# Inverting the first pair of chunks in 16x16 blocks joined by matmuls, with other PSUM banks and another early order, in a chunked delta-rule attention kernel

## The chip, the cores and the metric

One core of one Trainium2 chip. The metric is the device time of one launch in microseconds (us), given as the median of several runs; one further execution is profiled. TensorE (PE) multiplies matrices, VectorE (DVE) and ScalarE (ACT) work elementwise and move results out of PSUM, GpSimd (POOL) works elementwise beside DVE, SyncE (SP) issues transfers. PE's clock has two levels, 1.2 and 2.4 GHz; the profile shows the granted share of the higher one. All arithmetic is float32 or a split of a float32 number into two parts for the matmul.

## The reference

Three layers, one behind the other (sizes are batch 4, heads 8, 768 positions, head size 48; 3072 tokens of width 384):

```python
for t in range(S):                       # attention, per (batch, head)
    kt, vt, bt = k_n[:, :, t], v[:, :, t], beta[:, :, t, None]
    y[:, :, t] = einsum(q[:, :, t], state)
    state = state + bt * outer(kt, vt - state.T @ kt)
...
P = exp(x @ w_gate); 8 rounds of row and column normalisation
for e in range(8):                       # experts, 384 -> 1024 -> 384
    out += P[:, e:e+1] * (relu(x @ w1[e]) @ w2[e])
...
h = x @ w_in                             # 384 -> 2048
out = (h * cos(h)) @ w_out
```

## The kernel before, in words

The 768 positions are cut into 12 chunks of 64, called **units**; a unit holds its chunk of all 32 (batch, head) pairs. Inside a unit the recurrence is a lower triangular system of 64x64 per pair, done as two blocks of 32. Their inverses are made for two units at a time (units 0 and 1, 2 and 3, and so on): a tile holds one 32x32 system per partition and group, and `inv_ops` (L332 to L350) transposes the matrices into it (Nsys, L332), makes a unit triangle (L335, L339) and eliminates in 30 steps of a product (L346) and an addition (L350), 60 elementwise instructions. For the first pair all 60 run on DVE; for the later pairs they run on POOL, queued by the token `i`. `inv_dm` (L357) and `inv_tx` (L360) then transpose the inverse back into the tiles dm and tx.

The stages of a unit, with the letters that name them in the order string: T (L251, keys transposed, copied by ACT at L259), B (L277, Gram matrix of the keys; DVE and ACT combine the blocks at L302/L303, `gk_b` at L309 scales by beta, `gk_o` at L314 keeps the off-diagonal block Go), Q and q (queries transposed, and their Gram matrix, leaving DVE as Pp, L326), Z (`pe_Z1`, L368, dm times Go, copied out by ACT at L373), z (`pe_Z2`, L380, combined into Bs at L386 by ACT and L387 by DVE), K (`pe_KS`, L398, state times keys; DVE makes D from it at L414), k (L398, state times queries, "QS"), U (L426, out by DVE at L432), S (L441, state update at L446), P (L456, out by ACT at L461), X (L473, output transposed and split into two parts at L478/L479). `norm_sums` (L222 on ACT, L223 on DVE) and `norm_chain` (L231 to L238) make the keys' norms, `norm_scale` (L242) applies them; N is that chain for later units. G and g are the gate (L487, L491, and the small product L498).

K and q use the PSUM bank pair pab, Z1 and Z2 its two halves unless told otherwise: the D of a unit is read by DVE out of the bank that Z1 of the same unit writes next.

Everything up to unit 0's Z1 and Z2 is a hand-written prologue: loads on SP, ACT's and POOL's queues, sums and norms of units 0 and 1, their Gram products, the first inversion on DVE with parts of units 2 and 3 in between, POOL's inversion for units 2 and 3 (L335 on POOL), warm-up products on zeros (`warm`). Then `tick(u, seq)` walks a string of tokens for units 0 and 1 together, then for unit 2, then one string for odd and one for even units. Each engine takes its instructions in that order. The token m is one **half**: nine matmuls of 512 columns of expert 0, either the first layer h (L130, relu at L157/L158) or the second y (L151), on 512 tokens already through X, and a half is skipped when its tokens are not there yet (`done`). a, b and W split expert weights (L120 on ACT, L121 on DVE). Ahead of every token up to three queued POOL steps are emitted. Behind unit 11 the other experts follow, and then the last layer; that part takes most of the span and is the same in both kernels.

```python
elif c == "K":
    pe_KS(u)
elif c in "ZY":
    pe_Z1(u, *([p01[:, 0]] if early else []))
elif c == "r" and u + 1 < NU:
    inv_some(99)
    inv_dm(Xsys)
elif c == "i" and nxt["B"] < NU + 1 and u + 2 < NU:
    inv_q.extend(inv_ops(Nst, Nsys, Xsys, tmp, nc.gpsimd))
```

Of the kernel before, what the change touches and what calls it, by code (L numbers as in the profile page):

```python
# [34 lines left out]
def kernel(  # L35
# [555 lines left out]
    with tc.manual_schedule():  # L591
# [73 lines left out]
        gram(p23, KT[1], KT[1], True)  # L665
        n = [gk_n(0, pcd, n0), gk_n(1, p23, n0)]
        for u in range(2):
            gk_b(u, n[u], nc.vector)
        ops = inv_ops(n0, ns0, xs0, W0.rearrange("p s t -> p (s t)"), nc.vector)
        ops[0]()  # L670
        ops[1]()
        gk_o(0, pcd)
        gk_o(1, p23)
        for u in range(2, 4):
            norm_sums(u)
        for x in ops[2:8]:
            x()
        norm_chain(2, 4)
        for u in range(2, 4):
            norm_scale(u, nc.vector)  # L680
        nc.vector.transpose(out=beta_x, in_=bw[1].rearrange("p (u t) -> p u t", t=CB))
# [13 lines left out]
        pe_TQ(0, pab)  # L695
        load_q(1)
        pe_GQ(0, p01)
        for x in ops[14:]:
            x()
        inv_dm(xs0)  # L700
        inv_tx(xs0)
        warm(60)
        pe_KS(0)
        pe_Z1(0)
# [439 lines left out]
```

## Time and profile before

| | |
|---|---|
| median of 3 runs | 2311.76 us (2309.25 to 2312.98) |
| the profiled execution | 2312.32 us |
| its span | 2310.6 us, 37567 instructions |
| mean granted clock of PE | 0.972 |
| busy: PE, DVE, ACT, POOL | 2206.5 (95%), 996.1 (43%), 628.4 (27%), 476.3 (21%) |
| PE's busy tenths, first four of 40 slices (57.8 us each) | 5, 5, 7, 9 |

Times in the rows are us from the span's start. A line of a timeline reads: start, duration, engine, line of the kernel, operation, output<-inputs, shape, count of instructions in the row, and in brackets how long the engine stood idle before it and what released it. SPq is SP's queue of issued transfers. A line of the windows reads: stretch, its length, then the busy time (and count) of PE, PEld (weight loads), DVE, ACT and POOL, PE's granted clock as a share of 2.4 GHz, the busy share of the transfer engines, and GB/s. A line of the waits reads: who waited for whom, us in total, times, the longest.

### The profile page before, as it was taken

The numbers are of one execution on the slowest core, as the hardware profiler recorded it, in microseconds if no ns is written. First come the engines' busy times: TensorE is split into PE (matmuls) and PEld (weight loads), VectorE is DVE, ScalarE is ACT, GpSimd is POOL, SyncE is SP. The second block draws the span as 40 slices with busy tenths as digits, with TensorE's granted clock in tenths as the row PEclk, the third lists the DMA queues.
The fourth block names the chain that finished last, engine by engine and source line by source line (L and its number), as shares of the span: only waits on it lengthen the run. The fifth ranks groups of instructions, "written<-read, shape, count | busy, mean of one in ns | idle before, by whom it ended". The sixth has DMA issues, their size and how long they took to land.

```text
span 2310.6 us, 37567 instructions
## 1 busy us (share of the span) xinstructions
PE 2206.5 (95%) x16211; PEld 1843.4 (80%) x16211; DVE 996.1 (43%) x1613; ACT 628.4 (27%) x1017; POOL 476.3 (21%) x649
## 2 busy tenths in 40 slices
PE   5579999989999999999999999999999999999998
PEld 4467777768888888888888888888888878888887
DVE  7554452243235334334433433433232226666665
ACT  2233332231112112111111211211121126666565
POOL 5436445002122111111101110111011122221221
PEclk7789999999999999999999999999999999999999
DMA  4332322053212112101210211121021130000000
GB/s 80 84 77 64 78 71 55 32 191 118 73 42 81 34 37 78 41 29 50 78 32 28 85 40 37 49 61 37 17 69 41 60 110 1 14 14 14 15 14 14
DMA packets 167639, 123.87 MB, mean 54 GB/s; under 512 B 80208, under 2 KB 159568, under 8 KB 166704
## 3 DMA queue, kind: packets, MB, share of 16 engines
q1 hardware_dynamic: 161936, 97.36, 15.5%
q0 software_dynamic: 4448, 23.90, 3.0%
q8 instruction: 127, 2.08, 0.4%
q10 hardware_dynamic: 1088, 0.20, 0.1%
q14 instruction: 40, 0.33, 0.0%
HBM read 90.65 MB, written 30.77 MB: 53 GB/s over the span
## 4 chain that ended last, share of the span: by engine, by line
PE 90%; DVE 5%; issue 2%; ACT 2%; DMA 1%; POOL 0%; SPq 0%; POOLq 0%; ACTq 0%; DVEq 0%
PE ps L130 42%; PE ps L151 34%; PE ps L140 8%; PE ps L251 1%; PE ps L277 1%; PE ps L368 1%; PE ps L380 1%; PE ps L398 1%; DMA scr<-in_moe_w_dram 1%; DVE scr L350 1%; DVE W L346 1%; PE ps L426 0%; PE ps L652 0%; DMA ysc<-y 0%; DVE Nsys L332 0%
## 5 line engine op out<-in xcount | busy, mean ns | idle before, releaser
L130 PE MATMUL ps<-x,w1t 128*128 128x512 f32 x3564 | 877.5, 391 | 2.5 <-DVE h L158 1.4
L151 PE MATMUL ps<-h,w2t 128*128 128x512 f32 x3456 | 864.5, 395 | 0.0
L130 PEld LDWEIGHTS ps<-x,w1t 128*128 128x128 f32 x3564 | 669.0, 188 | 139.8 <-DVE h L158 2.1
L151 PEld LDWEIGHTS ps<-h,w2t 128*128 128x128 f32 x3456 | 654.7, 190 | 137.1
L158 DVE SCALAR_TENSOR_TENSOR h<-ps,h 128x512 fp32r<-128x512 f32 x384 | 265.5, 691 | 944.2 <-ACT h L157 944.1
L157 ACT ACTIVATE h<-ps 128x512 fp32r<-128x512 f32 x384 | 229.5, 598 | 1263.7 <-PE ps L130 1263.7
L939 POOL TENSOR_TENSOR acc<-acc,scr 128x512 f32<-128x512 f32 x126 | 165.9, 1317 | 1099.9 <-DVE scr L938 1099.9
L140 PE MATMUL ps<-w2t,h 128*128 128x384 f32 x720 | 138.5, 339 | 3.5 <-DVE acc L1019 1.5
L140 PEld LDWEIGHTS ps<-w2t,h 128*128 128x128 f32 x720 | 127.4, 188 | 13.2 <-ACT acc L1017 3.1
L995 DVE TENSOR_TENSOR tp<-tp,ps 128x512 f32<-128x512 f32 x96 | 66.1, 688 | 146.0 <-ACT tp L994 146.0
L130 PE MATMUL ps<-xb,w1t 128*128 128x512 f32 x432 | 113.7, 406 | 5.3 <-DVE xb L479 2.1
L981 POOL TENSOR_SCALAR tp<-tp 128x512 f32<-128x512 f32 x96 | 59.4, 619 | 256.8 <-ACT tp L980 256.6
L130 PEld LDWEIGHTS ps<-xb,w1t 128*128 128x128 f32 x432 | 79.5, 191 | 25.5 <-DVE xb L479 3.7
L938 DVE TENSOR_TENSOR scr<-ps,scr 128x512 f32<-128x512 f32 x126 | 86.0, 682 | 10.7 <-DMA scr<-pts 7.8
L140 PE MATMUL ps<-x,h 128*128 128x384 f32 x432 | 83.4, 339 | 0.0
L130 PE MATMUL ps<-x 128*128 128x512 f32 x324 | 81.8, 397 | 1.3 <-DVE scr L938 1.3
L1000 ACT ACTIVATE h<-tp 128x512 fp32r<-128x512 f32 x96 | 60.7, 632 | 76.9 <-DVE tp L995 70.2
L350 POOL TENSOR_TENSOR w1t<-w1t 128x30 f32<-128x30 f32 (+9 forms) x150 | 78.9, 526 | 11.8
L140 PEld LDWEIGHTS ps<-x,h 128*128 128x128 f32 x432 | 76.2, 188 | 5.6 <-DVE h L1005 2.4
L989 ACT ACTIVATE tp<-tp 128x512 f32<-128x512 f32 x96 | 60.7, 632 | 73.1 <-DVE tp L986 73.1
L346 POOL TENSOR_TENSOR w1t<-Nsys,w1t 128x30 f32<-128x30 f32 (+9 forms) x150 | 74.9, 500 | 11.3
L130 PEld LDWEIGHTS ps<-x 128*128 128x128 f32 x324 | 60.8, 189 | 12.8 <-DVE scr L938 1.6
(170 smaller groups left out, 1419.0 us busy)
## 6 DMA issues: line engine op xcount, KB each, us to landing
scr<-in_moe_w_dram SPq DMA_DIRECT2D x54, 384.0 KB
scr<-pts SPq DMA_DIRECT2D x48, 256.0 KB
xsc<-xb SPq DMA_DIRECT2D x24, 384.0 KB
x<-xsc POOLq DMA_DIRECT2D x6, 1536.0 KB, 7.9
tp<-in_moe_w_in_dram SPq DMA_DIRECT2D x16, 384.0 KB
wsa<-tp SPq DMA_DIRECT2D x32, 192.0 KB
tp<-in_moe_w_out_dram SPq DMA_DIRECT2D x16, 384.0 KB
wsb<-tp SPq DMA_DIRECT2D x32, 192.0 KB
```

Source lines behind the costliest of these rows:

```text
L130: nc.tensor.matmul(out=ps[:, :nn], lhsT=w[:, a, kk, fs], rhs=x[:, b, kk, c0:c0 + nn], start=(i == 0), stop=(i == 3 * KD - 1),)
L140: nc.tensor.matmul(out=ps[:, :DM], lhsT=h[:, a, ts], rhs=w[:, b, f % 2, :], start=(first and i == 0), stop=(last and i == 2),)
L151: nc.tensor.matmul(out=banks[kd], lhsT=w[:, a, f % 2, kd * 128:(kd + 1) * 128], rhs=h[:, b, :], start=(first and b == 0 and a == 0), stop= ...
L157: nc.scalar.activation(out=h[:, 0, :nn], in_=ps[:, :nn], func=ACTF.Relu)
L158: nc.vector.scalar_tensor_tensor(out=h[:, 1, :nn], in0=ps[:, :nn], scalar=0.0, in1=h[:, 0, :nn].bitcast(F32), op0=ALU.max, op1=ALU.subtract,)
L346: eng.tensor_tensor(out=a, in0=nsys[:, j + 1:, j:j + 1].to_broadcast([128, n, j]), in1=xsys[:, j:j + 1, 0:j].to_broadcast([128, n, j]), op ...
L350: eng.tensor_tensor(out=xsys[:, j + 1:, 0:j], in0=xsys[:, j + 1:, 0:j], in1=a, op=ALU.add)
L938: nc.vector.tensor_tensor(out=t, in0=ysets[n % 2][kd], in1=pb[e, b], op=ALU.mult)
L939: nc.gpsimd.tensor_tensor(out=acc[b][:, kd, :], in0=acc[b][:, kd, :], in1=t, op=ALU.add)
L989: nc.scalar.activation(out=rr[i % 2], in_=rr[i % 2], func=ACTF.Abs)
L995: nc.vector.tensor_tensor(out=c, in0=c, in1=hb2(i), op=ALU.mult)
L1000: nc.scalar.activation(out=h[:, 0], in_=c, func=ACTF.Copy)
```

## The change

The first pair's matrices are taken as 16x16 diagonal blocks: `inv16` eliminates both blocks of each 32x32 system at once in 14 steps (28 DVE instructions), and the block below the diagonal is then made on PE: `merge16_a` multiplies the original matrix by one block inverse, DVE scales it by a masked beta (ym), `merge16_b` multiplies by the other block inverse, and `merge16_c` adds the result into tx and transposes dm again. In the prologue the keys of unit 2 are issued ahead of beta, the norm chain of units 2 and 3 moves ahead of the first Gram products' combination, and POOL's inversion for units 2 and 3 is queued behind the merges. Z1 and Z2 take the bank pair pcd instead of pab. In the order strings N, T, Q, B, W and the gate of tick 0 move into tick 2, which has twelve halves instead of ten; unit 3 has a string of its own; the condition on `i` loses its first half, so that one more inversion is queued at unit 9.

```diff
-SEQ = ("U0 Y1 Q1 S0 P0 y1 K1 q1 k1 U1 X0 S1 P1 a0 N1 X1 T1 Q2 b0 B1 q2 G1 W1 g1",
+SEQ = ("U0 Y1 Q1 S0 P0 y1 K1 q1 k1 U1 a0 X0 S1 P1 X1 b0",
...
+    betam = ap1.tile([128, 2, NS], F32, name="betam")
-    hm = ap1.tile([128, 4], F32, name="hm")
+    hm = ap1.tile([128, 5], F32, name="hm")
...
+    def inv16(nst, nsys, xsys, tmp):
+        nc.vector.transpose(out=nsys, in_=nst.rearrange("p s t -> p t s"))
+        nc.gpsimd.affine_select(
+            out=xsys, in_=nsys, pattern=[[1, CB], [-1, CB]], compare_op=ALU.is_gt, fill=0.0, base=0,
+            channel_multiplier=0,
+        )
+        nc.gpsimd.memset(xsys.rearrange("p t i -> p (t i)")[:, 0:CB * CB:CB + 1], 1.0)
+        nc.gpsimd.memset(xsys[:, 16:32, 0:16], 0.0)
...
+        def step(j):
+            n = 15 - j
+            a = tmp[:, 0:2 * n * j].rearrange("p (a t i) -> p a t i", a=2, t=n)
+            x = blk(xsys, j + 1, 0, CB, 1, n, j)
+            nc.vector.tensor_tensor(
+                out=a, in0=blk(nsys, j + 1, j, CB, 0, n, j), in1=blk(xsys, j, 0, 0, 1, n, j), op=ALU.mult
+            )
+            nc.vector.tensor_tensor(out=x, in0=x, in1=a, op=ALU.add)
+
+        return [lambda j=j: step(j) for j in range(1, 15)]
+
+    def merge16_a(u, n, bank):
+
+        for s in range(NS):
+            for p in range(4):
+                r = slice(p * CB, p * CB + CB)
+                nc.tensor.matmul(
+                    out=bank[r, s * 16:s * 16 + 16], lhsT=n[r, u * NS + s, :], rhs=tx[r, u * NS + s, 16:32],
+                    start=True, stop=True, skip_group_check=True,
+                )
+        ym[u] = ap2.tile([128, NS, CB], F32, tag="W", name="ym")
+        nc.vector.tensor_tensor(
+            out=ym[u][:, :, 0:16], in0=bank[:, 0:NS * 16].rearrange("p (s t) -> p s t", t=16),
+            in1=betam[:, u, :, None].to_broadcast([128, NS, 16]), op=ALU.mult,
+        )
+
+    def merge16_b(u, bank):
...
+                    out=bank[r, (NS + s) * 16:(NS + s + 1) * 16], lhsT=dm[r, u * NS + s, :], rhs=y[r, s, 0:16],
...
+    def merge16_c(u, bank):
+        x = tx[:, u * NS:(u + 1) * NS, 16:32]
...
+        nc.vector.transpose(out=dm[:, u * NS:(u + 1) * NS, :], in_=tx[:, u * NS:(u + 1) * NS, :])
...
-    def pe_Z1(u, bank=pab[:, 0]):
+    def pe_Z1(u, bank=pcd[:, 0]):
-    def pe_Z2(u, bank=pab[:, 1]):
+    def pe_Z2(u, bank=pcd[:, 1]):
...
+        load_k(2)
         load_beta(0, nc.sync)
-        load_k(2)
...
+        for u in range(2, 4):
+            norm_sums(u)
         pe_TK(0, pab)
         pe_TK(1, p01)
         gram(pcd, KT[0], KT[0], True)
         gram(p23, KT[1], KT[1], True)
+        norm_chain(2, 4)
+        nc.vector.transpose(out=beta_sb, in_=bw[0].rearrange("p (u t) -> p u t", t=CB))
...
-        for x in ops[8:14]:
+        for x in ops:
             x()
+        inv_tx(xs0)
+        inv_dm(xs0)
+        pe_TQ(0, pab)
+        load_q(1)
+        warm_b(30)
+        merge16_a(0, n0, p01[:, 0])
+        merge16_a(1, n0, p01[:, 1])
+        n = [gk_n(2, pcd)]
+        merge16_b(0, p01[:, 0])
+        merge16_c(0, p01[:, 0])
+        n.append(gk_n(3, p23))
+        merge16_b(1, p01[:, 1])
+        merge16_c(1, p01[:, 1])
+        pe_KS(0)
+        pe_Z1(0, pab[:, 0])
+        pe_GQ_mms(0, p01)
         for u in range(2, 4):
             gk_b(u, n[u - 2], nc.vector)
+        gk_o(2, pcd)
         inv_q.extend(inv_ops(Nst, Nsys, Xsys, tmp, nc.gpsimd))
         inv_some(99)
-        gk_o(2, pcd)
+        pe_Z2(0, pab[:, 1])
+        pe_GQ_ev(0, p01)
         gk_o(3, p23)
...
-                elif c == "i" and nxt["B"] < NU + 1 and u + 2 < NU:
+                elif c == "i" and u + 2 < NU:
...
-        for u in range(3, NU):
-            tick(u, SEQ[2 + u % 2])
+        tick(3, SEQ[2])
+        for u in range(4, NU):
+            tick(u, SEQ[3 + u % 2])
```

**Where instructions stand now.** In these lists a row is one instruction or a run of like ones (x31), with the semaphores that it waits for; tile names carry buffer numbers. First ACT in the prologue, the sums (sq) and key copies (KT) of the first four units. Before:

```order
L232 ACTIVATE nrm<-nrm 128x32 [waits DVE_49]
L259 ACTIVATE KT<-ps_98 128x1024 [waits PE_49] x2
L302 ACTIVATE scr_133<-ps_98,hm 128x512 [waits PE_49,Pool_49]
L302 ACTIVATE scr_133<-ps_98,hm 128x512 [waits PE_49]
L222 ACTIVATE sq<-kr_129 128x768 [waits DMAHW4_49,DMAHW3_49,DMAHW5_49,DMAHW2_49,DMAHW6_49,DMAHW1_49,DMAHW7_49,DMAHW0_49,Activation_49]
L222 ACTIVATE sq<-kr_130 128x768 [waits DMASW4_49,DMASW3_49,DMASW5_49,DMASW2_49,DMASW6_49,DMASW1_49,DMASW7_49,DMASW0_49,DVE_49]
L232 ACTIVATE nrm<-nrm 128x32 [waits DVE_49]
```

And now:

```order
L225 ACTIVATE sq<-kr_129 128x768 [waits DMAHW0_49,DMASW3_49,DMAHW1_49,DMASW2_49,DMAHW2_49,DMASW1_49,DMAHW3_49,DMASW0_49,DVE_49]
L235 ACTIVATE nrm<-nrm 128x32 [waits DVE_49]
L225 ACTIVATE sq<-kr_130 128x768 [waits DMAHW4_49,DMAHW3_49,DMAHW5_49,DMAHW2_49,DMAHW6_49,DMAHW1_49,DMAHW7_49,DMAHW0_49,Activation_49]
L225 ACTIVATE sq<-kr_131 128x768 [waits DMASW4_49,DMASW3_49,DMASW5_49,DMASW2_49,DMASW6_49,DMASW1_49,DMASW7_49,DMASW0_49,DVE_49]
L262 ACTIVATE KT<-ps_98 128x1024 [waits PE_49] x2
L235 ACTIVATE nrm<-nrm 128x32 [waits DVE_49]
L305 ACTIVATE scr_134<-ps_98,hm 128x512 [waits PE_49,Pool_49]
```

The sums of units 2 and 3 (kr_129, kr_130 before; kr_130, kr_131 now) stood behind the first key copies and first combinations (scr); now they stand ahead of the copies, and so does their chain ahead of the combinations.

Second, DVE from the end of the first inversion to U of unit 0. Before:

```order
L350 TENSOR_TENSOR scr_133<-scr_133,W_134 128x2x29 [waits DVE_49]
L346 TENSOR_TENSOR W_134<-scr_133 128x30 [waits DVE_49]
L350 TENSOR_TENSOR scr_133<-scr_133,W_134 128x30 [waits DVE_49]
L357 STREAM_TRANSPOSE dm<-scr_133 128x32x32 [waits DVE_49,Pool_49]
L360 STREAM_TRANSPOSE tx<-scr_133 128x32x32
L387 SCALAR_TENSOR_TENSOR Bs<-ps_98,hm,Bs 128x16x32 [waits PE_49,Activation_49]
L823 TENSOR_TENSOR wg<-wg_sb,wg 128x3x8 [waits DMAHW0_49]
L432 TENSOR_TENSOR U<-ps_98,beta_x 128x2x8x48 [waits PE_49]
```

Now the last elimination step (112 elements at most in any) is followed by both transposes and the two ym products; from the second unit's merge on it reads:

```order
L306 SCALAR_TENSOR_TENSOR w2t<-ps_98,hm,w2t 128x512 [waits Activation_49]
L417 TENSOR_TENSOR tx<-tx,ps_98 128x16x16 [waits PE_49]
L420 STREAM_TRANSPOSE dm<-tx 128x512 [waits DVE_49]
L312 TENSOR_TENSOR w2t<-w2t,beta_sb 128x512 x2
L317 TENSOR_TENSOR Go<-ps_98,beta_sb 128x512
L341 STREAM_TRANSPOSE Nsys<-w2t 128x1024 [waits DVE_49]
L455 SCALAR_TENSOR_TENSOR Bs<-ps_98,hm,Bs 128x16x32 [waits PE_49,Activation_49]
L335 TENSOR_TENSOR Pp<-ps_98,mask 128x1024
L317 TENSOR_TENSOR Go<-ps_98,beta_sb 128x512
L785 STREAM_TRANSPOSE beta_x<-bw 128x384 [waits DMASW4_49,DMASW5_49,DMASW3_49,DMASW6_49,DMASW2_49,DMASW7_49,DMASW1_49,DMASW0_49]
L908 TENSOR_TENSOR wg<-wg_sb,wg 128x3x8 [waits DMAHW0_49,Activation_49]
L500 TENSOR_TENSOR U<-ps_98,beta_x 128x2x8x48 [waits DVE_49,PE_49]
```

The combinations, scales, Nsys, Go and Pp of units 2 and 3, which stood inside the old elimination, and beta_x now stand between the inversion and U.

Third, PE at the start of unit 4. Before:

```order
L398 MATMUL ps_98<-S_125,KT 64x48 [waits DVE_49]
L398 MATMUL ps_98<-S_125,KT 64x48 x31
L368 MATMUL ps_98<-dm,Go 32x32 [waits DVE_49]
L368 MATMUL ps_98<-dm,Go 32x32 x31
L151 MATMUL ps_98<-h,w2t 128x512 x9
L380 MATMUL ps_98<-tx,W 32x32 [waits Activation_49]
L380 MATMUL ps_98<-tx,W 32x32 x31
L130 MATMUL ps_98<-xb,w1t 128x512 x9
L398 MATMUL ps_98<-S_125,QT 64x48 x32
L426 MATMUL ps_98<-D,Bs 64x48 [waits DVE_49]
```

And now:

```order
L466 MATMUL ps_98<-S_126,KT 64x48 [waits DVE_49]
L466 MATMUL ps_98<-S_126,KT 64x48 x31
L436 MATMUL ps_98<-dm,Go 32x32 [waits DVE_49]
L436 MATMUL ps_98<-dm,Go 32x32 x31
L131 MATMUL ps_98<-xb,w1t 128x512 [waits DVE_49]
L131 MATMUL ps_98<-xb,w1t 128x512 x8
L448 MATMUL ps_98<-tx,W 32x32 [waits DVE_49,Activation_49]
L448 MATMUL ps_98<-tx,W 32x32 x31
L152 MATMUL ps_98<-h,w2t 128x512 x9
L466 MATMUL ps_98<-S_126,QT 64x48
L466 MATMUL ps_98<-S_126,QT 64x48 [waits DVE_49]
L466 MATMUL ps_98<-S_126,QT 64x48 x30
```

Z1 (L368, now L436) waited for DVE's D, the last reader of its bank; its wait now is the one for dm, which is there in even units alone, and the second matmul of QS (L466 with QT) waits for Bs on DVE instead.

## Rows read from the trace of the kernel before

**Rows 1.** The page: its first line, and the chain of waits by engine.

```profile
span 2310.6 us, 37567 instructions
...
PE 90%; DVE 5%; issue 2%; ACT 2%; DMA 1%; POOL 0%; SPq 0%; POOLq 0%; ACTq 0%; DVEq 0%
```

**Rows 2.** Windows by stage: start:end, us, busy us (count) of PE, PEld, DVE, ACT, POOL, PEclk.

```profile
28.60:71.10 42.50, 17.70 (x276) 14.69 (x276) 39.36 (x79) 4.68 (x6) 21.78 (x40) 0.66 0.16 38
...
80.60:100.60 20.00, 16.43 (x660) 14.77 (x658) 7.87 (x9) 6.26 (x9) 2.32 (x9) 0.83 0.53 115
...
100.50:170.40 69.90, 52.09 (x919) 41.54 (x918) 37.53 (x57) 22.94 (x34) 16.50 (x30) 0.83 0.39 101
...
170.40:205.70 35.30, 32.37 (x685) 25.83 (x684) 18.23 (x24) 12.26 (x19) 20.38 (x37) 1.00 0.32 80
```

**Rows 3.** Timeline of DVE in the prologue: start us, duration us, line, operation, count.

```profile
28.64 0.19 DVE L346 TENSOR_TENSOR W<-scr 128x30 f32<-128x30 f32 x1
...
30.79 0.30 DVE L346 TENSOR_TENSOR W<-scr 128x130 f32<-128x130 f32 x1
...
41.54 1.60 DVE L303 SCALAR_TENSOR_TENSOR w2t<-ps,hm,w2t 128x512 f32<-128x512 f32 x2
...
46.21 1.24 DVE L314 TENSOR_TENSOR Go<-ps,beta_sb 128x512 f32<-128x512 f32 x2
...
64.60 0.63 DVE L346 TENSOR_TENSOR W<-scr 128x130 f32<-128x130 f32 x1
...
71.11 1.94 DVE L357 STREAM_TRANSPOSE dm<-scr 128x1024 f32<-128x1024 f32 x1
...
80.59 0.96 DVE L432 TENSOR_TENSOR U<-ps,beta_x 128x768 f32<-128x768 f32 x1 [1.99 <-PE ps L426]
```

**Rows 4.** Window of DVE alone, beside the old elimination loop: us, busy us (count), PEclk.

```profile
41.54:48.51 6.97, 6.83 (x10) 0.86 0.31 59
```

**Rows 5.** SP's queue in the prologue, then landing times of the key loads.

```profile
12.48 5.95 SPq L206 DMA_DIRECT2D kr<-in_k_dram  x8
...
DMA to landing us min/median/max: 2.2/2.3/3.8
```

**Rows 6.** Timeline of PE, units 2 and 3.

```profile
126.20 1.91 PE L368 MATMUL ps<-dm,Go 32*32 32x32 f32 x64 [3.23 <-DVE dm L357]
...
158.53 1.94 PE L251 MATMUL ps<-ident,kr 128*128 128x128 f32 x8 [6.12 <-issue]
...
172.74 1.20 PE L368 MATMUL ps<-dm,Go 32*32 32x32 f32 x64 [1.15 <-DVE D L414]
...
173.87 2.33 PE L151 MATMUL ps<-h,w2t 128*128 128x512 f32 x9
```

**Rows 7.** Waits of PE from 168 to 480 us: us in total, times, longest.

```profile
PE ps L368 <- DVE D L414: 12.8, 9, 2.0
```

**Rows 8.** Timeline of PE, start of unit 4.

```profile
205.72 1.15 PE L398 MATMUL ps<-S,KT 48*64 48x48 f32 x64
...
208.63 1.92 PE L368 MATMUL ps<-dm,Go 32*32 32x32 f32 x64 [1.76 <-DVE D L414]
...
210.47 3.90 PE L151 MATMUL ps<-h,w2t 128*128 128x512 f32 x9
```

**Rows 9.** Windows of unit 4's tick, its first wait, and unit 11's tick.

```profile
206.00:240.00 34.00, 32.06 (x682) 26.15 (x678) 14.69 (x21) 9.15 (x15) 28.29 (x52) 0.90 0.27 61
...
207.00:209.00 2.00, 0.37 (x14) 0.38 (x16) 1.57 (x2) 0.00 (x0) 1.19 (x1) 0.51 0.03 8
...
442.00:474.00 32.00, 29.29 (x533) 22.90 (x525) 7.64 (x10) 8.40 (x14) 0.00 (x0) 0.95 0.15 51
```

**Rows 10.** Timeline of POOL: start and end of its first inversion.

```profile
46.36 1.26 POOL L335 TENSOR_SCALAR_AFFINE_SELECT w1t<-Nsys 128x1024 f32<-128x1024 f32 x1 [19.98 <-DMA qr<-in_q_dram]
...
83.05 0.19 POOL L826 TENSOR_TENSOR two<-ident 16x8 f32<-16x8 f32 x1
```

**Rows 11.** Timeline of PE: the gate's small product ahead of unit 4.

```profile
204.74 1.05 PE L498 MATMUL ps<-two,w2t 16*128 16x8 f32 x8 [1.15 <-ACT w2t L494]
```

More of the change, by code (lines that the diff above doesn't have):

```diff
@@ L306, in gk_n, with gk_b @@
         return n
-    def gk_b(u, n, eng):
-        eng.tensor_tensor(out=split_i(n), in0=split_i(n), in1=sbg(u, CB), op=ALU.mult)
+    def gk_b(u, n, eng, out=None):
+        eng.tensor_tensor(out=split_i(n if out is None else out), in0=split_i(n), in1=sbg(u, CB), op=ALU.mult)
     def gk_o(u, bank):
@@ L323, in pe_GQ, with pe_GQ_mms, pe_GQ_ev @@
     def pe_GQ(u, bank=pab):
+        pe_GQ_mms(u, bank)
+        pe_GQ_ev(u, bank)
+    def pe_GQ_mms(u, bank):
         gram(bank, KT[u], QT[u], False)
+    def pe_GQ_ev(u, bank):
         Pp[u] = ap2.tile([128, NS, C], F32, tag="Pp", name="Pp", bufs=1)
@@ L354, in inv_ops, with blk @@
         return ops
+    def inv16(nst, nsys, xsys, tmp):
[6 more added lines that the diff above has]
+        nc.gpsimd.memset(xsys[:, 16:32, 0:16], 0.0)
+        def blk(t, t0, i0, dt, di, n, j):
+            a = t[:, t0:t0 + 1, i0:i0 + 1]
+            return bass.AP(a.tensor, a.offset, [a.ap[0], [16 * CB + 16, 2], [dt, n], [di, j]])
+        def step(j):
[7 more added lines that the diff above has]
+        return [lambda j=j: step(j) for j in range(1, 15)]
@@ new lines, in merge16_b @@
+    def merge16_b(u, bank):
+        y = ym.pop(u)
+        for s in range(NS):
+            for p in range(4):
+                r = slice(p * CB, p * CB + CB)
+                nc.tensor.matmul(
+                    out=bank[r, (NS + s) * 16:(NS + s + 1) * 16], lhsT=dm[r, u * NS + s, :], rhs=y[r, s, 0:16],
+                    start=True, stop=True, skip_group_check=True,
+                )
+    def merge16_c(u, bank):
+        x = tx[:, u * NS:(u + 1) * NS, 16:32]
+        nc.vector.tensor_tensor(
+            out=x, in0=x, in1=bank[:, NS * 16:2 * NS * 16].rearrange("p (s t) -> p s t", t=16), op=ALU.add
+        )
+        nc.vector.transpose(out=dm[:, u * NS:(u + 1) * NS, :], in_=tx[:, u * NS:(u + 1) * NS, :])
@@ L356, in inv_dm @@
+    ym = {}
     def inv_dm(xsys):
@@ L599 @@
         bw = [t.rearrange("p t i -> p (t i)")[:, 0:NU * CB] for t in (Xsys, Nsys)]
+        bw[1] = hp.tile([128, 2, 512], F32, tag="h", name="bw")[:, 0, 0:NU * CB]
         for t in bw:
@@ L632 @@
                 nc.gpsimd.memset(hm[p0:p0 + CB, 2 + hf:3 + hf], -1.0)
+                nc.gpsimd.memset(hm[p0:p0 + 16, 4:5], 1.0)
         load_k(3, nc.gpsimd, nc.gpsimd)
@@ L647, in inv_some, with warm_b @@
                 inv_q.pop(0)()
+        def warm_b(n):
+            for i in range(n):
+                nc.tensor.matmul(out=p01[:, i % 2, 0:256], lhsT=zero[:, 0:128], rhs=zero, start=True, stop=True)
         def warm(n):
@@ L660 @@
             norm_scale(u, nc.vector)
-        nc.vector.transpose(out=beta_sb, in_=bw[0].rearrange("p (u t) -> p u t", t=CB))
+        for u in range(2, 4):
+            norm_sums(u)
         pe_TK(0, pab)
@@ L665 @@
         gram(p23, KT[1], KT[1], True)
+        norm_chain(2, 4)
+        nc.vector.transpose(out=beta_sb, in_=bw[0].rearrange("p (u t) -> p u t", t=CB))
         n = [gk_n(0, pcd, n0), gk_n(1, p23, n0)]
         for u in range(2):
[L668 to L681, printed above, removed]
+            gk_b(u, n[u], nc.vector, xs0[:, u * NS:(u + 1) * NS, :])
+        ops = inv16(xs0, ns0, xs0, W0.rearrange("p s t -> p (s t)"))
+        for u in range(2):
+            norm_scale(2 + u, nc.vector)
+            nc.vector.tensor_scalar(
+                out=betam[:, u].rearrange("p (i m) -> p i m", i=2),
+                in0=beta_sb[:, u, 0:NS].rearrange("p (m i) -> p i m", i=2), scalar1=hm[:, 4:5], scalar2=None,
+                op0=ALU.mult,
+            )
+            gk_o(u, (pcd, p23)[u])
         pe_TK(2, pab)
@@ L685 @@
         gram(p23, KT[3], KT[3], True)
-        for x in ops[8:14]:
+        for x in ops:
             x()
-        n = [gk_n(2, pcd), gk_n(3, p23)]
+        inv_tx(xs0)
[14 more added lines that the diff above has]
+        pe_GQ_mms(0, p01)
         for u in range(2, 4):
             gk_b(u, n[u - 2], nc.vector)
+        gk_o(2, pcd)
         inv_q.extend(inv_ops(Nst, Nsys, Xsys, tmp, nc.gpsimd))
         inv_some(99)
-        gk_o(2, pcd)
+        pe_Z2(0, pab[:, 1])
+        pe_GQ_ev(0, p01)
         gk_o(3, p23)
[L695 to L704, printed above, removed]
+        nc.vector.transpose(out=beta_x, in_=bw[1].rearrange("p (u t) -> p u t", t=CB))
         nc.scalar.activation(out=wg[:, :, 0, :], in_=wg_sb, func=ACTF.Copy)
-        pe_Z2(0)
         xblk, xq, bigp, scr = {}, [], [], []
@@ L801, in tick @@
                         pe_GQ(n, p01 if early else pab)
+                elif c == "E":
+                    pe_TQ(u)
+                    load_q(u + 1)
+                elif c == "e":
+                    pe_GQ(u)
                 elif c == "X":
@@ L809, in tick @@
                     inv_tx(Xsys)
-                elif c == "i" and nxt["B"] < NU + 1 and u + 2 < NU:
+                elif c == "i" and u + 2 < NU:
                     inv_q.extend(inv_ops(Nst, Nsys, Xsys, tmp, nc.gpsimd))
-                elif c in "Gg" and u % 2:
-                    (pe_gate if c == "G" else pe_gate2)(u // 2)
+                elif c in "Gg":
+                    (pe_gate if c == "G" else pe_gate2)((u - 1) // 2)
                 elif c in "ab":
```

3 rows, old and new, of the table SEQ are left out of this document.

## The prediction

> **What bounds the kernel now.** First the page's head and chain [rows 1]: of a span of 2310.6 us TensorE (PE) is in 90% of the chain that ends last, VectorE (DVE) in 5%. So time is won only where PE waits or runs slowly, and the next view is the windows by stage [rows 2]. From 28.60 to 71.10 PE is busy for 17.70 of 42.50 us, DVE for 39.36: DVE inverts the first group's matrices and PE has nothing else. From 80.60 to 170.40 PE's granted clock is 0.83, and 17.81 of the 69.90 us behind 100.50 are idle. From 170.40 to 205.70 the clock is 1.00 and PE is busy for 32.37 of 35.30. Third, the waits of PE from unit 3 on [rows 7]: Z1 (L368) stands nine times for DVE's D (L414), 12.8 us in all. Fourth, PE's timeline of unit 4 [rows 8]: behind the 1.76 us wait Z1 takes 1.92 and the next expert half 3.90, where unit 3, after a 1.15 wait, has 1.20 and 2.33 [rows 6]. In the windows [rows 9] the clock is 0.51 from 207 to 209, 0.90 over unit 4's tick.
>
> The sum is made against the profiled execution, 2312.32 us (span 2310.6); the median of the three runs shown is 2311.76, 0.56 lower. A difference of 0.2% (4.6 us) is about what a measurement tells from none.
>
> **A. The first inversion, up to DVE's U of unit 0 (at 80.59 now [rows 3]).** SP issues unit 2's keys ahead of beta; they are issued now from 12.48 on for 5.95 us, behind eight beta transfers, and land 2.2 to 3.8 us after issue [rows 5]. In front of them they would be issued by about 12.5 and land at 14.8 to 16.4. The squares, sums and norm chain of units 2 and 3 now stand ahead of the first Gram products on ACT and DVE; counting those off behind the landing, the first elimination pair starts at about 31.1, where it starts at 28.64 now [rows 3]. The bounds are 28.6 (no delay) and 32.0 (latest landing): a loss of 0 to 3.4, taken 2.5.
>
> Gone are 60 elementwise operations of 30 to 240 elements a partition; 28 come, all of 112 at most. A pair of 30 elements takes two of 0.19 and gaps, 0.47, one of 130 two of 0.30 and gaps, 0.66; the 0.63 for the same 130 elements at 64.60 stands where GpSimd (POOL) is running too [rows 3], and POOL's inversion now starts later than this stretch. 14 pairs at 0.56 end at 38.9 (bounds 37.7 to 41). Two full transposes at 1.94 [rows 3]: 42.7.
>
> Then DVE works in order through what now lies before U: the eight instructions that it did inside the old loop (combinations, scales, Nsys, Go, Pp for units 2 and 3), 6.83 [rows 4]; two half transposes, 1.94; ym and the addition for each unit, four of 256 elements, between the 0.30 of 130 elements and the 0.62 of a Go of 512 (1.24 for two), taken 0.4, so 1.6; one Bs like one of the pair at 41.54, 0.75 [rows 3]; 1.4 for gaps and the two short ones, beta_x and wg. That is 12.5. It stands for PE's merge products in between. These are 256 float32 matmuls, two passes each, 512 passes. Their nearest row is Z1 at full clock: 64 passes in 1.20 us, 18.75 ns each [rows 6]; at half clock 1.92, 30 ns [rows 8]. A block of 128 is 2.4 us; with unit 2's and 3's combination between them DVE stands 4.3. U of unit 0 comes at 42.7 + 12.5 + 4.3 = 59.5, **21.1 earlier**. At 30 ns it is 5 less. The far bound is the gate's small product, eight in 1.05 us, 131 ns each [rows 11], each alone with a long weight load: 57 us more. I take 18.75, since 32x32 tiles in a stream are what the merges are.
>
> The Trainium skill, TensorEngine Tiling (Array Packing), section Instruction Overhead, speaks against so many narrow products: about 60 cycles each, and one column costs as much as 60. At 2.4 GHz I work out from it an estimate of 25 ns, 12.8 us for the 512, 3.2 more than by the row. The row's 18.75 ns disagrees with it, and I go by the row.
>
> What covered what: warm-up products are halved, and POOL's affine_select and two fills lie beside the scales of units 2 and 3. The small additions (fifth column of hm, betam, a moved beta buffer) are costed at nothing: they lie on POOL and DVE beside transfers ahead of the first pair; without that cover they would be well under 1 us.
>
> **B. U0 to the end of X1.** Same work, 20.0 us now, 16.43 busy at 0.83 [rows 2]: 13.6 at full clock. Going in behind a stretch where PE is fed, I keep some 2.1 of idle time and 1.2 of slow clock: 16.9, **3.1 less**, bounds 0 and 5.
>
> **C. X1 to unit 4's first product (100.5 to 205.72 now [rows 8]).** N, T, Q, B of units 2 and 3 and the first gate leave tick 0, and tick 2 gets twelve expert halves instead of ten; tick 3 gives up one. Work at full clock now: 52.09 at 0.83 is 43.2, and 32.37 at 1.00, together 75.6 [rows 2]; stalls and slow clock are the other 29.6. Among them are 3.23 for dm before Z1 of unit 2 and 6.12 before a key transpose at 158.53 [rows 6]. The change does one half more, 2.33 (at 173.87 [rows 6]): 77.9. Its first half needs X1's split, so a wait stays there; KS of unit 2 will wait on DVE behind the norm chain, a weight split and Pp, about 5; dm again about 3.5; slow clock behind each; tick 3's own. I count 20.2, so 98.1 and **7.1 less**. Bounds: 29.6 as now (a loss of 2.3) and some 10 (a gain of 17).
>
> **D.** The half done early is a half that tick 5 no longer has to do: **2.3**.
>
> **E. Units 4 to 11.** Z1 and Z2 write pcd instead of pab, and Z1 no longer waits for D. The waits are 12.8 [rows 7]; unit 3's 1.15 [rows 6] is in C, so 11.65. The slow clock behind them: in unit 4 Z1 loses 0.72 and the half 1.57, 2.3 [rows 6, 8]. The clock is like unit 4's 0.90 in four ticks and like unit 11's 0.95 in two [rows 9]: 4 times 2.3 and 2 times 1.5, 12.2. I take four fifths, 9.8, since other short waits stay: **21.5**, bounds 0 (the wait only moves) and 23.9.
>
> A sixth inversion at the end of unit 9's tick, which nobody reads, adds a transpose on DVE and some 37 us of POOL work. POOL has no work there that PE waits for; were that cover gone, Nsys' transpose would delay one D by 1.94, and D no longer gates Z1.
>
> Sum: 21.1 + 3.1 + 7.1 + 2.3 + 21.5 = 55.1. 2312.3 less 55.1 is 2257.2 in a profiled execution; less 0.56, **2257**.
>
> **The rivals.**
> 1. *The clock falls anyway.* For: in unit 3 a wait of 1.15 did not lower it [rows 6], in unit 4 one of 1.76 stands at the fall [rows 8, 9], so the fall may belong to thin work ahead rather than to the wait. E is then the waits alone, 11.7, and the time 2267. The Trainium skill, TensorE: Matmul & The Clock Gate, section Why this matters for your kernels, wants only PE gaps over about 3 us avoided; by that rule gaps of 1.76 would not be what lowers it, and the time would be this rival's. The trace has it lowered right at such a gap, so the rule gets no more than 0.15.
> 2. *POOL becomes the bound.* Its first inversion takes 36.7 us (46.36 to 83.05 [rows 10]), is now started behind the merges at about 56 and ends at about 93, ahead of the first gate; the second ends near the time at which unit 4's dm is wanted, while the ticks have become shorter. If it ends late, C gives nothing: 2264. Chance 0.14.
> 3. *The wait moves.* QS of a unit now stands for the second Bs on DVE, which lies behind D and Nsys. If the slack (an expert half, 2.33, against 0.75 and the rest of D) doesn't hold, E shrinks to 0 to 10: 2268 to 2278. Chance 0.10.
> 4. *Slower: merges at the price of single products.* At 131 ns a pass, the 512 cost 57 more than I count and eat all; beyond 0.126 us (55.1 / 512 over 18.75 ns) the change loses, at 0.14 it is 2319. For it: 16 columns are too narrow to hide a weight load. Against: every 32x32 row. Chance 0.06.
>
> **How the numbers follow.** Forecast 0.55, then 0.15, 0.14, 0.10, 0.06. The range goes from 2238 (stalls of C near 10, the pairs at 0.47, the whole of E) to 2280 (rival 3's end). Faster by over 0.2%: all but rival 4, 0.95; within: 0.02; slower: 0.03.
>
> **What would show it.** U of unit 0 on DVE near 59.5; 14 pairs in about 8 us; merge blocks of 128 passes at 2.4; X1's end near 76.5, unit 4's first product near 174.5; no wait of Z1 for D in the list and a clock of 1.00 in unit 4's tick; POOL's first inversion ending near 93; a sixth at unit 9. A clock still at 0.90 there makes rival 1; PE waiting for dm or for the gate's small operand, rival 2; QS waiting for Bs, rival 3; merge blocks over 10 us, rival 4.

## The result, and the profile after

The changed kernel takes 2271.47 us (median of four runs, 2269.81 to 2272.74) beside 2310.94 for the kernel before on the same chip: ratio 0.9828, 95% interval 0.9811 to 0.9845. That is 39.5 us less. It lies inside the range of 2238 to 2280, 14 us above the 2257 forecast: the sign and most of the gain came; three terms of the sum (A, B and C) were too large.

The page of the changed kernel: the first line, then PE's granted clock in 40 slices, then the chain of waits by engine.

```profile
span 2269.8 us, 38558 instructions
...
PEclk7789999999999999999999999999999999999999
...
PE 91%; DVE 4%; issue 2%; ACT 1%; DMA 1%; POOL 1%; SPq 0%; POOLq 0%; DVEq 0%; ACTq 0%
```

Against [rows 1] the span is 40.8 shorter, though the program has some thousand instructions more: the merge products. The slices are too coarse to say more, so the stages are read off at the same four instructions in both traces. First DVE in the prologue:

```profile
32.05 0.19 DVE L383 TENSOR_TENSOR W<-scr 128x28 f32<-128x28 f32 x1
...
39.88 1.92 DVE L428 STREAM_TRANSPOSE tx<-scr 128x1024 f32<-128x1024 f32 x1
41.66 1.89 DVE L425 STREAM_TRANSPOSE dm<-scr 128x1024 f32<-128x1024 f32 x1
43.42 0.40 DVE L400 TENSOR_TENSOR ym<-ps,betam 128x256 f32<-128x256 f32 x1
46.42 0.42 DVE L400 TENSOR_TENSOR ym<-ps,betam 128x256 f32<-128x256 f32 x1 [2.60 <-PE ps L395]
...
50.16 0.42 DVE L417 TENSOR_TENSOR tx<-tx,ps 128x256 f32<-128x256 f32 x1 [2.66 <-PE ps L410]
...
53.89 0.42 DVE L417 TENSOR_TENSOR tx<-tx,ps 128x256 f32<-128x256 f32 x1 [1.93 <-PE ps L410]
...
60.49 0.75 DVE L455 SCALAR_TENSOR_TENSOR Bs<-ps,hm,Bs 128x512 f32<-128x512 f32 x1 [1.80 <-PE ps L448]
...
63.56 0.96 DVE L500 TENSOR_TENSOR U<-ps,beta_x 128x768 f32<-128x768 f32 x1
```

The first elimination pair starts at 32.05, the 14 pairs take 7.8 us, and U of unit 0 starts at 63.56 where it started at 80.59 [rows 3]: 17.0 earlier. Four waits for PE, 9.0 us, stand between the transposes and U: three for the merges, 7.2, and one for Z2 of unit 0, 1.8.

Then PE: the end of X1, and the waits up to unit 4.

```profile
83.20 0.87 PE L541 MATMUL ps<-ident,Y 128*128 128x128 f32 x6 [0.99 <-ACT Y L529]
...
100.20 1.96 PE L466 MATMUL ps<-S,KT 48*64 48x48 f32 x64 [5.00 <-DVE Pp L335]
...
117.40 1.52 PE L436 MATMUL ps<-dm,Go 32*32 32x32 f32 x64 [3.23 <-DVE dm L425]
...
165.07 1.31 PE L254 MATMUL ps<-ident,kr 128*128 128x128 f32 x8 [2.43 <-DVE S L514]
...
175.74 1.67 PE L254 MATMUL ps<-ident,kr 128*128 128x128 f32 x8 [3.13 <-issue]
178.52 1.98 PE L280 MATMUL ps<-QT,KT 48*64 48x64 f32 x64 [1.11 <-ACT KT L262]
...
191.66 1.15 PE L466 MATMUL ps<-S,KT 48*64 48x48 f32 x64
192.74 1.20 PE L436 MATMUL ps<-dm,Go 32*32 32x32 f32 x64
193.87 2.34 PE L131 MATMUL ps<-xb,w1t 128*128 128x512 f32 x9
```

Unit 4 starts at 191.66, 14.1 earlier than at 205.72 [rows 8], so the gain shrinks from 17.0 to 14.1 on the way. In unit 4 itself Z1 follows its state product at once, at 1.20, and the half behind it takes 2.34 (1.92 and 3.90 in [rows 8]). The windows from X1's end to unit 4, and from there to the last small product of the last gate, in the changed kernel (columns as in [rows 2]):

```profile
84.07:191.66 107.59, 88.20 (x1612) 69.99 (x1612) 53.36 (x80) 35.46 (x53) 49.81 (x90) 0.87 0.38 91
...
191.66:433.44 241.78, 235.33 (x5040) 190.14 (x5039) 106.26 (x133) 73.45 (x115) 131.47 (x252) 0.99 0.25 65
```

And in the kernel before:

```profile
100.54:205.72 105.18, 84.44 (x1602) 67.37 (x1602) 55.74 (x81) 35.17 (x53) 36.88 (x66) 0.89 0.36 94
...
205.72:473.01 267.29, 249.26 (x5049) 200.32 (x5048) 103.54 (x132) 73.50 (x115) 99.91 (x190) 0.94 0.23 59
```

So units 4 to 11 take 25.5 less, at a clock of 0.99 instead of 0.94. PE's idle time there falls from 18.0 to 6.5 (window less busy time), and its busy time by 13.9, of which 2.3 is the half that is no longer done there; the rest, 11.6, is the clock. The waits of [rows 7] are gone; the longest entry of the same list is now

```profile
PE ps L131 <- ACT xb L546: 1.8, 2, 0.9
```

The stretch ahead of unit 4 takes 2.4 more. By stage, profiled execution against profiled execution:

| stage | forecast | measured |
|---|---|---|
| A, up to U of unit 0 | -21.1 | -17.0 |
| B, to the end of X1 | -3.1 | +0.6 |
| C, to unit 4 | -7.1 | +2.4 |
| D and E, units 4 to 11 | -23.8 | -25.5 |
| behind it | 0 | -1.2 |

The table compares one execution with one. C in particular varies: three kernels below whose edits lie outside C (the first merge product twice, no sixth inversion, beta first) took 108.19, 104.87 and 104.35 for it, where the changed kernel took 107.59. Against 105.18 before, C comes to something between -0.8 and +3.0, and no gain beyond that spread is shown.

### The profile page after: what moved, and what is told of

Its sections match the earlier page's. It is cut to its first block, busy times and chain, and to the rows that moved or that the text cites. A ratio compares the mean times of both kernels' runs of the same rounds, so it can differ in the third digit from the quotient of the medians.

```text
span 2269.8 us, 38558 instructions
## 1 busy us (share of the span) xinstructions
PE 2199.6 (97%) x16693; PEld 1841.9 (81%) x16693; DVE 976.7 (43%) x1590; ACT 628.1 (28%) x1017; POOL 512.3 (23%) x716
## 4 chain that ended last, share of the span: by engine, by line
PE 91%; DVE 4%; issue 2%; ACT 1%; DMA 1%; POOL 1%; SPq 0%; POOLq 0%; DVEq 0%; ACTq 0%
PE ps L131 42%; PE ps L152 34%; PE ps L141 8%; PE ps L466 1%; PE ps L280 1%; PE ps L254 1%; PE ps L436 1%; PE ps L448 1%; PE ps L494 1%; DMA scr<-in_moe_w_dram 0%; PE ps L541 0%; PE ps L509 0%; PE ps L524 0%; POOL kr L209 0%; DMA ysc<-y 0%
## 5 line engine op out<-in xcount | busy, mean ns | idle before, releaser
L131 PEld LDWEIGHTS ps<-xb,w1t 128*128 128x128 f32 x432 | 80.5, 193 | 25.5 <-DVE xb L547 3.5
L359 POOL TENSOR_TENSOR w1t<-w1t 128x30 f32<-128x30 f32 (+9 forms) x180 | 96.7, 537 | 14.1
L355 POOL TENSOR_TENSOR w1t<-Nsys,w1t 128x30 f32<-128x30 f32 (+9 forms) x180 | 89.4, 497 | 13.6
```

What stands on the lines that cost most here:

```text
L131: nc.tensor.matmul(out=ps[:, :nn], lhsT=w[:, a, kk, fs], rhs=x[:, b, kk, c0:c0 + nn], start=(i == 0), stop=(i == 3 * KD - 1),)
L355: eng.tensor_tensor(out=a, in0=nsys[:, j + 1:, j:j + 1].to_broadcast([128, n, j]), in1=xsys[:, j:j + 1, 0:j].to_broadcast([128, n, j]), op ...
L359: eng.tensor_tensor(out=xsys[:, j + 1:, 0:j], in0=xsys[:, j + 1:, 0:j], in1=a, op=ALU.add)
```

## The experiments

Two groups of four kernels, each group timed beside the kernel before on one chip (2310.82 for the first, 2309.76 for the second). The changed kernel itself was in neither group, so a difference from it has that difference between groups, about 1 us, in it.

**The bank alone, and the bank taken back.** The kernel before with

```diff
-    def pe_Z1(u, bank=pab[:, 0]):
+    def pe_Z1(u, bank=pcd[:, 0]):
-    def pe_Z2(u, bank=pab[:, 1]):
+    def pe_Z2(u, bank=pcd[:, 1]):
...
-        pe_Z1(0)
+        pe_Z1(0, pab[:, 0])
-        pe_Z2(0)
+        pe_Z2(0, pab[:, 1])
```

> The kernel before with one part of the change: Z1 and Z2 from unit 2 on write pcd instead of pab. Theory (the bank is worth the waits for D and the slow clock behind them): between unit 4's first product and the gate's last small product PE took 267.3 us in the kernel before and 241.8 in the changed one, 25.5 less, of which 2.3 is the half done early; so 23.2 here, 1.2 more for unit 3's wait, 24.4 less: 2286.5. Rival (the clock falls for another reason): the waits alone, 12.8 less: 2298. Rival (the bank does nothing without the new order): 2311.

It took 2287.13 (2285.54 to 2293.64), ratio 0.9904, interval 0.9877 to 0.9930: 23.7 less, and 24.4 was expected. The changed kernel with the first two edits reversed:

> The changed kernel with Z1 and Z2 back in pab. Theory: 24.4 more than the changed kernel, 2296, with the waits for D back in the list (some 12 us) and a clock near 0.9 in the even ticks. Rival (clock for another reason): 2284. Rival (the early order needs the new bank too): 2300 or more.

It took 2294.23 (2290.98 to 2299.50), ratio 0.9931, interval 0.9908 to 0.9953: 22.8 above the changed kernel. Its list of PE's waits from unit 4 to the last gate has the old wait again:

```profile
PE ps L436 <- DVE D L482: 13.3, 8, 2.6
```

and its windows of units 4 and 5 have clocks of 0.90 and 0.94, where the bank alone has 1.00 in unit 4's tick (the third row is the kernel of the bank alone):

```profile
194.00:229.00 35.00, 31.09 (x641) 25.41 (x634) 16.22 (x23) 9.52 (x14) 28.73 (x52) 0.90 0.26 59
229.00:260.00 31.00, 29.31 (x662) 22.93 (x661) 14.37 (x22) 10.02 (x15) 5.45 (x12) 0.94 0.32 77
```

```profile
206.00:240.00 34.00, 33.93 (x807) 27.88 (x803) 16.29 (x24) 11.61 (x18) 28.21 (x51) 1.00 0.28 64
```

Both ways the edit is worth about 23 us where the waits that it removes are 12.8 (13.3 in the kernel with the bank taken back). From unit 4's first product to the last gate the bank alone takes

```profile
205.84:450.90 245.06, 239.89 (x5050) 193.89 (x5049) 102.79 (x132) 73.54 (x115) 99.91 (x190) 0.98 0.25 64
```

22.2 less than the kernel before: 12.9 of idle time and 9.4 of busy time for the same matmuls. Taken back it is 24.1 more (265.90 against 241.78), 12.8 idle and 11.3 busy. The busy part is the clock, which rises when these waits go and falls when they return; that settles the first rival. Not every wait brings it down: in the kernel before Z1 or the half behind it ran slowly after six of the nine, among them one of 1.08, and not after three, among them one of 1.26, so the length alone does not decide. The edit needs neither the new inversion nor the new strings.

**The old strings on the new prologue.** The two tables of strings and the loop over units from the kernel before:

```diff
-SEQ = ("U0 Y1 Q1 S0 P0 y1 K1 q1 k1 U1 a0 X0 S1 P1 X1 b0",
+SEQ = ("U0 Y1 Q1 S0 P0 y1 K1 q1 k1 U1 X0 S1 P1 a0 N1 X1 T1 Q2 b0 B1 q2 G1 W1 g1",
...
-        tick(3, SEQ[2])
-        for u in range(4, NU):
-            tick(u, SEQ[3 + u % 2])
+        for u in range(3, NU):
+            tick(u, SEQ[2 + u % 2])
```

> The changed kernel with the order strings of the kernel before: N, T, Q, B, W and the gate back in tick 0, ten halves in tick 2, unit 3 on the odd string. New inversion, prologue and banks stay. Theory 1 (the new strings gave nothing: X1 to unit 4 took 107.6 us after and 105.2 before): 2272, within 3. Theory 2 (the strings are what lets the earlier X1 count, since POOL's inversion now ends at 96 and the old tick 0 wants the gate and the second inversion earlier): 2278 to 2287.

It took 2268.66 (2264.78 to 2274.50), ratio 0.9820, interval 0.9796 to 0.9844: not distinguishable from the changed kernel, and if anything below it. X1 to unit 4 and units 4 to 11 read:

```profile
82.84:186.98 104.14, 83.77 (x1603) 67.19 (x1602) 56.83 (x81) 35.29 (x53) 49.13 (x91) 0.87 0.37 93
...
186.98:428.06 241.08, 235.47 (x5049) 190.68 (x5049) 104.72 (x133) 73.66 (x115) 131.46 (x252) 1.00 0.25 65
```

So the first theory holds, though the median lies 0.3 below its band of 2269 to 2275: no gain from the strings shows. C takes 104.14 here, with one half less done; 3.5 less than in the changed kernel, but the runs with the changed strings reach down to 104.35 and up to 108.19, so the strings make no difference that shows. Units 4 to 11 take as long with that half (288 matmuls of the second expert layer there against 279) as without; the half's 2.3 us can't be seen, at a clock of 1.00 here and 0.99 in the changed kernel's window.

**The first merge product twice.**

```diff
-        for s in range(NS):
+        for s in [s for s in range(NS) for _ in range(2)]:
             for p in range(4):
```

> The changed kernel with every matmul of the first merge product done twice, 256 more passes of 16 columns. Theory (PE's narrow products there are bound by the loading of its instructions: gaps of 1.8 to 2.0 us with no releaser, one for some 128 passes, a 16 KB instruction transfer every 3.6 us): two more gaps, 28.5 ns a pass, 7.3 more: U of unit 0 on DVE at 70.9 instead of 63.6 and 2279. Rival (the price is the engine's own, 9.4 ns a pass at full clock or 14.8 at half): 2.4 to 3.8 more, U at 66 to 67.4. Rival (the row of Z1, 18.75 ns): 4.8 more, U at 68.4.

It took 2278.38 (2276.01 to 2282.12), ratio 0.9861, interval 0.9842 to 0.9881: 6.9 more than the changed kernel. U of unit 0 starts 6.9 later. That is 27 ns for each of the 256 added passes. That U on DVE, then PE's timeline of this kernel:

```profile
70.43 0.96 DVE L500 TENSOR_TENSOR U<-ps,beta_x 128x768 f32<-128x768 f32 x1
```

```profile
42.36 1.86 PE L395 MATMUL ps<-tx,scr 32*32 32x16 f32 x200
46.20 1.55 PE L395 MATMUL ps<-tx,scr 32*32 32x16 f32 x128 [1.98 <-issue]
49.66 1.90 PE L395 MATMUL ps<-tx,scr 32*32 32x16 f32 x128 [1.90 <-issue]
53.11 0.94 PE L395 MATMUL ps<-tx,scr 32*32 32x16 f32 x56 [1.55 <-issue]
53.88 1.14 PE L410 MATMUL ps<-ym,dm 32*32 32x16 f32 x72
56.84 1.90 PE L410 MATMUL ps<-ym,dm 32*32 32x16 f32 x128 [1.83 <-issue]
```

200 passes go through in 1.86 us, 9.3 ns each, and then PE stands with no releaser once for every 128 passes: 128, 128, then 56 and 72, then 128. In the changed kernel the same gaps stand in the chain of waits between 30 and 90 us (start, us, what):

```profile
41.85 1.89 PE ps L395 x123
43.74 1.96 issue
45.70 0.63 PE ps L395 x47
46.33 0.94 PE ps L410 x47
47.26 1.89 issue
49.15 1.91 PE ps L410 x128
51.06 1.82 issue
```

and in the transfers of 42 to 54 us the queue that loads instructions is the only one at work, 16 KB at a time (the first row is all packets of the window):

```profile
DMA packets 3, 0.05 MB, mean 4 GB/s; under 512 B 0, under 2 KB 0, under 8 KB 0
...
q8 instruction: 3, 0.05, 1.5%
```

A pass is a weight load and a matmul, 128 passes are 256 instructions, and one load of 16 KB is seen for each. The three packets pass at 43.3, 46.8 and 50.5, some 0.5 us ahead of a gap, and PE goes on 2.4 us behind each; in the kernel with the product twice its five gaps end 2.4 to 2.6 us behind a packet. That fits a stream that runs at the rate at which its instructions come. The rates of 9.4 and 14.8 ns fall as the price of an added pass, and the row of Z1 at 18.75 with them.

**The sixth inversion left out.**

```diff
-                elif c == "i" and u + 2 < NU:
+                elif c == "i" and nxt["B"] < NU + 1 and u + 2 < NU:
```

> The changed kernel with the old condition on the token i, so that the sixth inversion, which nobody reads, is not queued. Theory (it lies on POOL beside work that PE doesn't wait for): 2271, within 2. Rival (its transpose on DVE or POOL's 37 us delay a unit): 2 to 5 less, 2267 to 2269.

It took 2267.40 (2266.11 to 2268.75), ratio 0.9812, interval 0.9793 to 0.9832, which overlaps that of the changed kernel. The median, 4.1 lower, is the rival's (2267 to 2269). But its profile is 2.7 ahead at unit 4 already, long before that inversion is queued at unit 9, and 2.8 at the last gate (430.65 against 433.44):

```profile
188.97 1.15 PE L466 MATMUL ps<-S,KT 48*64 48x48 f32 x64
```

So the inversion itself costs nothing that shows in the traces; ahead of unit 4 the two programs are the same, and their executions differ by that much.

**Pp ahead of the norm chain.** In unit 2's string:

```diff
-"m E m N W e m N K G m g T m B m r Z R m W z T m k U m S P B i m X m W Q q m",
+"m E m e N W m N K G m g T m B m r Z R m W z T m k U m S P B i m X m W Q q m",
```

> The changed kernel with one token of unit 2's string moved: the Gram product of queries and keys (e) stands ahead of the norm chain and the weight split (N, W), so that DVE makes Pp before them. PE's order is the same. Theory (the state product of unit 2 waits 5.0 us for Pp, which stands behind N and W on DVE, and PE's clock falls behind that wait): the state product starts at 95 instead of 100.2, 5 to 7 less: 2265. Rival (the wait moves: the keys of unit 4 or the experts' weights are late by as much, or POOL, which ends its inversion at 96, sets it): 0 to 2 less.

It took 2266.44 (2263.50 to 2272.36), ratio 0.9804, interval 0.9781 to 0.9827. The state product of unit 2 starts at 95.37, as the theory has it, and the 5.0 us wait is gone. But its profiled execution (2272.36, the slowest of the four) reaches unit 4 at 191.24, only 0.4 earlier:

```profile
95.37 1.15 PE L466 MATMUL ps<-S,KT 48*64 48x48 f32 x64
...
99.40 1.89 PE L131 MATMUL ps<-xb,w1t 128*128 128x512 f32 x7 [0.93 <-DVE w1t L122]
102.16 1.02 PE L566 MATMUL ps<-two,w2t 16*128 16x8 f32 x8 [0.87 <-ACT w2t L562]
104.88 1.73 PE L254 MATMUL ps<-ident,kr 128*128 128x128 f32 x8 [1.69 <-DVE D L482]
...
116.28 1.92 PE L436 MATMUL ps<-dm,Go 32*32 32x32 f32 x64 [3.23 <-DVE dm L425]
```

3.5 of it comes back in three waits, and dm is late as before. C takes 106.94, inside the spread of the runs without this edit. The median alone is the theory's, the profile is the rival's: inconclusive by itself.

**Three moves together.** The strings of units 2 and 3:

```diff
-"m E m N W e m N K G m g T m B m r Z R m W z T m k U m S P B i m X m W Q q m",
-"K Z m z m k U N m S P T m X B N m Q T q m B r m R G m i g",
+"m E m e N W m N K r R G m g T m B m Z m W z T m k U m S P B i m X m W Q q N m",
+"K Z m z m k U m S N P T m X B m Q T q m B r m R G m i g",
```

> The changed kernel with three moves of tokens, PE's order the same: e ahead of N and W (as in the run beside it); the two transposes of POOL's inverse (r, R) right behind the state product of unit 2, ahead of the halves, where they stood behind an expert half's split on DVE; and the norm chains of unit 3's string one place each earlier, the first at the end of unit 2's string, the second behind the state update. Theory (what C lost are waits behind DVE's order: 5.0 for Pp, 3.2 for dm, 2.4 for S behind a norm chain, 3.1 and 1.1 for a late norm chain, and slow clock behind each): all gone, 12 to 18 less than the changed kernel, 2254 to 2259, with unit 4's first product near 175. Rival (POOL's inversions are the bound there once these go): dm of unit 4 is late and half of it comes back, 2263.

It took 2254.80 (2253.21 to 2258.26), ratio 0.9760, interval 0.9739 to 0.9780: 16.7 below the changed kernel, 55 below the kernel before, the fastest here. From X1's end to unit 4:

```profile
83.01:175.14 92.13, 80.15 (x1613) 63.42 (x1612) 53.66 (x79) 34.82 (x53) 49.65 (x91) 0.98 0.43 107
...
111.46 1.20 PE L436 MATMUL ps<-dm,Go 32*32 32x32 f32 x64
...
153.50 1.09 PE L254 MATMUL ps<-ident,kr 128*128 128x128 f32 x8 [0.17 <-DVE S L514]
```

92.1 us instead of 107.6 (104.4 at the least in the other runs with the changed kernel's strings), on the same PE work in the same order, at a clock of 0.98 instead of 0.87. Dm is there when Z1 wants it, S's readers wait 0.17 instead of 2.43. POOL does not become the bound: Z1 of unit 4 starts at 176.22, right behind its state product. The three moves were not tried one by one, except the first.

**Beta first again.**

```diff
-        load_k(2)
         load_beta(0, nc.sync)
+        load_k(2)
```

> The changed kernel with the old order of the first loads on SP: beta ahead of the keys of unit 2. Theory (the head now hangs on those keys: sums, copies, combination follow their landing): issue 5.8 us later, the first elimination pair at 37 to 38 instead of 32.05, and since narrow products follow without slack, 5 to 6 more: 2277. Rival (the keys are covered by the first key copies and the norm chain of units 0 and 1): within 2 of 2271.

It took 2274.39 (2272.46 to 2277.11), ratio 0.9843, interval 0.9823 to 0.9864: 2.9 more than the changed kernel, with intervals that overlap, and 7.0 more than the kernel without the sixth inversion, which was timed in the same group. Its first elimination pair starts at 36.81, 4.8 later, and U of unit 0 at 67.86, 4.3 later; DVE stands for the squares of those keys:

```profile
21.56 0.95 DVE L226 TENSOR_REDUCE nrm<-sq 128x16 f32<-128x768 f32 x1 [6.00 <-ACT sq L225]
```

So the head hangs on these keys, as the first theory says; in the changed kernel and the six others with its prologue the first pair stands between 30.5 and 32.05. At unit 4 this run is 1.3 behind the changed kernel (192.92) and 4.0 behind the run without the sixth inversion, whose C (104.87) is as long as the one here (104.35). How much of the delay reaches the end is thus open between 3 and 7 us.

**What is not isolated.** The changed kernel is 15.7 below the bank alone. The strings and the sixth inversion show no part in that, so it belongs to the new inversion and the new order of the prologue together; the keys' place is 3 to 7 of it. No run has the old inversion in the new prologue, so what the 16x16 blocks are worth by themselves is not shown.

## Why the prediction was right or wrong, point by point

**How the time came into the range.** A, B and C were too large by 4.1, 3.7 and 9.5; D with E was 1.7 too small, and behind unit 11 1.2 less came that nobody forecast. B and C came out at the bad ends of their own bounds (0 and a loss of 2.3). That 2271 lies in the range is in part luck: its upper end, 2280, was set by rival 3, which did not come. The lower end, 2238, does not follow from the three terms named for it; they give about 2243.

**E held.** The waits for D are worth nearly twice their own length because the clock falls behind most of them. The forecast of 21.5 for units 4 to 11 stands beside 22.2 by the bank alone and 24.1 taken back, and the 9.8 taken for the slow clock beside 9.4 and 11.3. The clock rival (chance 0.15) and the third (QS waits for Bs) fell: in units 4 to 11 no wait for Bs is in the list. D's 2.3 by itself is not shown: with the old strings the half is back in units 4 to 11, and they take no longer.

The Trainium skill, TensorE: Matmul & The Clock Gate, section Why this matters for your kernels, asks that PE gaps over about 3 us be avoided. These gaps were 2.6 us at most, and taking them away raised the clock in unit 4's tick from 0.90 to 1.00: the measurement decides against leaving gaps of that size alone.

**A was 4.1 too large, B 3.7.** The step that failed is the price of a merge pass, 18.75 ns from the row of Z1. The merges ran from 41.85 to 53.82, 12.0 us (23 ns a pass) for 512 passes with what stands between, and the run with 256 more gives 27 ns a pass. The bound that I took for PE's own rate hid another: in [rows 6] and [rows 8] a Z1 of 64 passes stands beside wide products, where there is time for its instructions to come (argued, not tried); the merges are 512 passes in a row. DVE stood for PE for 9.0 us where 4.3 were forecast: 7.2 for the merges, and 1.8 for Z2, narrow products behind them at half clock, for which the sum had nothing. 0.7 more had gone at the end of the transposes (43.4 against 42.7: the first pair started at 32.05 where 31.1 was forecast; over the runs it lies on both sides of that), and DVE's own work behind them took 11.1 of the 20.1 us to U where 12.5 was forecast: 4.7 + 0.7 - 1.4 make the 4. B goes on with stages of 64 narrow passes: 3.3 of its 20.5 us are idle where 2.1 was kept, 2.3 of it in two gaps with no releaser, and the slow clock cost 3.6 (17.22 busy beside 13.6) where 1.2 was kept. I gave it credit for a fed PE; it came in with the clock at half, 0.50 from the merges' second gap at 47.26 on, and has 0.75 from 63.56 to 84.07. The direction of rival 4 was right, then: merges cost more than their row, but far from the 131 ns of [rows 11].

The Trainium skill, TensorEngine Tiling (Array Packing), section Instruction Overhead, has about 60 cycles for each narrow matmul; at 2.4 GHz I estimated 25 ns from it. That came nearer to the cost in a long stream than the row did. But 200 passes at 9.3 ns each disagree with it as a price of a pass between gaps, though a single pass lasts 0.18 us there; here 27 ns comes from gaps, so that the estimate came near is luck.

**C was 9.5 too large.** The step that failed is "I count 20.2" of stalls and slow clock. By the same work of 77.9 it was 29.7 (26.5 to 30.3 in the other runs), as much as the 29.6 before: 19.4 idle, the rest a clock of 0.87. I had the wait for Pp (about 5, it was 5.00) and for dm (3.5, it was 3.23), but left "tick 3's own" without a price, and unit 3 has 2.43, 3.13 and 1.11 and slow clock behind each, since a norm chain stands ahead of the state update on DVE and the second comes late. That the waits are DVE's order and not POOL or the amount of work is shown by the three moves, which won back 12 to 16 us with the same PE order. The old strings gave the same time as the new: they have a wait of 5.67 ahead of a key transpose in tick 0, and the new ones 5.00 for Pp in tick 2 instead.

**POOL.** Its first inversion ended at 96.2 (forecast 93), ahead of the first gate, and Z1 of unit 4 did not wait for dm; rival 2 did not come. The 3.23 for dm in unit 2, which stood there before too, went with the three moves of DVE's order. The sixth inversion cost nothing, as said.

## What to carry to other kernels

Where a small wait recurs ahead of narrow work, look at the clock behind it: here nine waits of 1.1 to 2.0 us cost nearly as much again, though three of them left the clock alone, and a PSUM bank that its last reader leaves earlier was worth 23 us of the 40. Before a difference of 3 us in one stretch is explained, look at that stretch in other runs of the same code. When elementwise steps are exchanged for many narrow matmuls, price them by a stretch in which as many follow each other, not by a short group between wide ones. And a token moved from a stall to another place brings its wait along if the engine that serves it takes its work in order: look at what it queues behind there.
